# Projecting the queries' last 64 rows as row-tiled pairs, six tiles to a bank, in a recurrent-memory transformer kernel

## The chip, the cores and the metric

The kernel runs on one core of a Trainium2 chip. The metric is the device time of one execution in microseconds; the time before is the median of three runs. A profiled execution of the same program gives the trace.

## The reference

Two layers of a memory-augmented attention block and a gated feed-forward block, over 2048 tokens of 448 features. The attention block goes through 64 segments of 32 tokens one after another, because the first 8 output rows of a segment are the memory of the next:

```
for s in range(64):
    h = concat([mem, x[:, 32*s:32*s+32]])          # 40 rows of 448
    q, k, v = h @ Wq, h @ Wk, h @ Wv               # 16 heads of 256
    p = softmax(where(mask, q @ k.T / 16, -1e9))
    o = (p @ v) @ Wo
    mem, out_s = o[:, :8], o[:, 8:]
x = x + attention(layernorm(x)); x = x + (relu(g @ W_gate) * (g @ W_up)) @ W_down   # g = layernorm(x), twice
```

## The kernel before

The prologue multiplies the weights together per head: A = Wq Wk^T (448 x 448) and B = Wv Wo. So scores are (h A) h^T and the output is (p h) B, and k and v are never formed. A is kept in A_sb: the 448 input rows are four parts of 128 rows, the fourth having 64 rows and zeros. Heads come in two halves (hf 0 and 1) of eight. The 448 output rows of eight heads make 28 tiles of 128 (NT), numbered t; tiles 24 to 27 hold two heads' last 64 rows each.

Two chains run side by side, layer one at segment g and layer two at segment g - 4 (LAG). A step g handles both: 68 steps, of which g = 4 to 63 have both chains and 80 moving columns (two times 40), the others one chain and 40. After every second step a Feed (odd g) runs the feed-forward block of 64 tokens per layer.

TensorE's instructions are issued strictly in the order in which the program names them (`in_order`, line 73). The other engines' order is set by the scheduler when the program is built, and each engine then works through its own list in that order. PSUM has eight banks: seven in rotation (tag "ps") and one (tag "ox", bufs=1) that gathers the step's output.

One step on TensorE, in order: `project` of half 0 (h A, 28 tiles times four parts, evacuated to TQ and TZ by VectorE and ScalarE, groups of four tiles and 320 columns); `hk_make` (transposes h); `project` of half 1 with `scores_m(0)` (scores of the memory rows, tile Sm) between; `flipped` (transposes PM, the memory rows' probabilities, through PSUM tile pps into PT); `scores_x` (Sx: first a matmul that writes the mask, then 16 of 40 columns); `weigh_m` (ya, yb, from PT); the same for half 1; `project_out` (ox, 28 tiles times four); `weigh_x` (the other rows' y, from 40-row operands that sit on rows 0 to 39 and 64 to 103). At the end of a step `finish` reads ox: VectorE copies the new memory into the next h (`set_mem`, line 193), ScalarE copies the rest to OT (line 606).

`weights_of` (line 479) is the softmax: maximum (mx), subtraction (se), exponential on ScalarE, sum (ssum), reciprocal (rs), product.

The last part of h stands twice, on rows 0 to 63 and again on 64 to 127 (B_sb has 512 columns for that). `project_early` (line 434) uses it: eight of the 56 last-part matmuls of the next step, for tiles u = 6 and u = 0 of half 0, are issued as four pairs on upper and lower 64 rows, inside `weigh_x`, before the step's first full matmul. The other 48 are full-height matmuls over 64 rows of weights and 64 rows of zeros, in `project` (line 449).

Of the kernel before, what the change touches and what calls it, by code (L numbers as in the profile page):

```python
# [19 lines left out]
MEM = 8  # L20
# [13 lines left out]
W = 2 * L  # L34
XO = (0, 2 * L - SEG)
M0 = SEG
HX = (0, 64 + MEM)
HM = (SEG, 64)


EARLY = (6, 0)


def upper(hf, u):

    return hf == 0 and u == 0

# [6 lines left out]
def build_kernel(ctx, tc, A_x, A_mem0, A_Wq, A_Wk, A_Wv, A_Wo, B_W_gate, B_W_up, B_W_down, out,  # L54
# [79 lines left out]

    A_sb = glob.tile([P, 4, 2, NT, 128], BF, name="A_sb")
    B_sb = glob.tile([P, 2, NT, 512], BF, name="B_sb")
# [59 lines left out]
    with tc.tile_pool(name="pre", bufs=6) as pre:  # L196
# [4 lines left out]
        for i in range(6):  # L201
            t = pre.tile([P, 4, 512], BF, name=f"nat{i}", bufs=1)
            (nc.gpsimd if i % 2 else nc.vector).memset(t[64:128, 3, :], 0.0)
            nats.append(t)
        nc.gpsimd.memset(A_sb[64:128, 3, :, :, :], 0.0)
        nc.gpsimd.memset(A_sb[0:64, 3, 0, 0:4, :], 0.0)
        for t in TQ + TZ + PX + PM + YB:
# [60 lines left out]
        for p in range(NP):  # L268
# [4 lines left out]
            for kd in range(4):  # L273
                for eo in range(2):
                    aps = psum.tile([P, 3, 128], F32, tag="ps", name="aps")
                    for t in range(2):
                        e = 2 * eo + t
                        mm(aps[:, :, :], qT[:, e, kd * 128:(kd + 1) * 128],
                           kT[:, e, 0:384], start=(t == 0), stop=(t == 1))
                    for t in range(2):  # L280
                        e = 2 * eo + t
                        mm(mx_ps[:, kd, eo * 64:eo * 64 + 64], qT[:, e, kd * 128:(kd + 1) * 128],
                           kT[:, e, 384:448], start=(t == 0), stop=(t == 1))
                    t0 = eo * 4 + p4
                    if kd < 3:
                        share(A_sb[:, kd, hf, t0:t0 + 17:8, :], aps[:], 384, (1.28, 0.85))
                    elif upper(hf, eo):
                        share(A_sb[64:128, 3, hf, t0, :], aps[64:128, 0, :], 128, (1.28, 0.85))
                        share(A_sb[0:64, 3, hf, t0 + 8:t0 + 17:8, :], aps[0:64, 1:3, :], 256, (1.28, 0.85))
                    else:  # L290
                        share(A_sb[0:64, 3, hf, t0:t0 + 17:8, :], aps[0:64], 384, (1.28, 0.85))
                if todo:
                    todo.pop(0)()
            share(A_sb[:, 0:3, hf, 24 + p4, :], mx_ps[:, 0:3, :], 384, (1.28, 0.85))
            share(A_sb[0:64, 3, hf, 24 + p4, :], mx_ps[0:64, 3, :], 128, (1.28, 0.85))
            if p == 2:
# [55 lines left out]
    Wd_sb = main.tile([P, FT, DM], BF, name="Wd_sb")  # L352
    for dst, src in ((Wg_sb, B_W_gate), (Wu_sb, B_W_up)):
        nc.gpsimd.memset(dst[64:128, 3, :], 0.0)
        nc.sync.dma_start(dst[:, 0:3, :], src[0:384].rearrange("(k p) n -> p k n", p=P))
        nc.sync.dma_start(dst[0:64, 3, :], src[384:448])
    nc.sync.dma_start(Wd_sb[:], B_W_down.rearrange("(f p) d -> p f d", p=P))

# [74 lines left out]

    def project_early(chains, hb, j):

        n = L * len(chains)
        pre = {u: psum.tile([P, 512], F32, tag="ps", name="prj") for u in EARLY}
        low = [(u, p4) for u in EARLY for p4 in range(4) if not upper(0, u)]
        up = [(u, p4) for u in EARLY for p4 in range(4) if upper(0, u)]
        seen = set()  # L440
        for pair in zip(low, up):
            for u, p4 in pair:
                rows = slice(64, 128) if upper(0, u) else slice(0, 64)
                mm(pre[u][:, p4 * n:(p4 + 1) * n], A_sb[rows, 3, 0, 4 * u + p4, :],
                   moving(hb, j, 3, chains, rows), start=(u not in seen), stop=False, skip_group_check=True)
                seen.add(u)
        return pre

    def project(hf, chains, hb, j, us, pre={}):

        n = L * len(chains)
        for u in us:
            ps = pre[u] if u in pre else psum.tile([P, 512], F32, tag="ps", name="prj")
            for p4 in range(4):
                for kd in range(3 if u in pre else 4):
                    mm(ps[:, p4 * n:(p4 + 1) * n], A_sb[:, kd, hf, 4 * u + p4, :], moving(hb, j, kd, chains),
                       start=(kd == 0 and u not in pre), stop=(kd == (2 if u in pre else 3)),
                       skip_group_check=u in pre)
            if u < 6:
                parts = [(nc.scalar if u % 2 else nc.vector, slice(0, P), TQ[hf][:, :, u, :])]  # L460
            else:
                parts = [(nc.vector, slice(0, 64), TZ[hf][0:64, :, 0:64]),
                         (nc.scalar, slice(64, 128), TZ[hf][64:128, :, 64:128])]
            for eng, rows, T in parts:
                T = T.rearrange("p g (t q) -> p t g q", q=16)
                if len(chains) == 2:
                    evac(eng, T, ps[rows, 0:4 * n].rearrange("p (t g q) -> p t g q", t=4, q=16))
                    continue
                c = chains[0]
                src = ps[rows, 0:4 * n].rearrange("p (t w) -> p t w", t=4)  # L470
                x, m = (0, SEG) if c == 0 else (MEM, 0)
                evac(eng, T[:, :, 2, MEM * c:MEM * c + MEM], src[:, :, m:m + MEM])
                evac(eng, T[:, :, 3 * c:3 * c + 2, :],
                     src[:, :, x:x + SEG].rearrange("p t (g q) -> p t g q", q=16))

    def queries(hf, g, kd):
        return TQ[hf][:, g, 2 * kd:2 * kd + 2, :] if kd < 3 else TZ[hf][:, g, :]

    def weights_of(Sp, n, dst, keep, tag):

        mx = main.tile([P, n], F32, tag=f"mx{tag}", name="mx")
        nc.vector.tensor_reduce(mx[:], Sp[:], axis=AX.X, op=ALU.max)
        se = main.tile([P, n, L], F32, tag=f"se{tag}", name="se")
        nc.vector.tensor_tensor(se[:], Sp[:], mx[:].unsqueeze(2).to_broadcast([P, n, L]), op=ALU.subtract)  # L484
# [20 lines left out]
    def step(g, ff, pre):  # L505
# [6 lines left out]
        lo, hi = min(a for a, _ in cols), max(b for _, b in cols)  # L512
        ox = psum.tile([P, 4, W], F32, tag="ox", bufs=1, name="ox")

# [18 lines left out]
        def scores_x(hf):  # L533
            Sp = psum.tile([P, 4, L], F32, tag="ps", name="Sx")
            mm(Sp[:, :, :], ident[:], maskS[:], start=True, stop=False, skip_group_check=True)
            for half in range(2):
                for c in chains:
                    for kd in range(4):
                        mm(Sp[:, 2 * half + c, :], queries(hf, 3 * c + half, kd), moving(hb, j, kd, (c,)),
                           start=False, stop=(half == 1 and c == chains[-1] and kd == 3), skip_group_check=True)  # L540
            return Sp

        def probs_x(hf, Sp):
            weights_of(Sp, 4, PX[hf], None, f"x{hf}")

# [13 lines left out]
        def weigh_x(hf, hk, PT, then=None):  # L559

            def keep(eng, c, t0, src):
                n = src.shape[-1] // SEG
                dst = YB[hf][:, t0:t0 + n, XO[c]:XO[c] + SEG]
                k = max(1, n // 8)
# [26 lines left out]
        def project_out(hf, t0, t1):  # L591

            for t in range(t0, t1):
                for mc in range(4):
# [4 lines left out]
        def finish():  # L599
            if ms:  # L600
                src = ox[:, :, M0:M0 + 16].rearrange("p k (c m) -> p k c m", m=MEM)
                set_mem(g + 1, src[:, :, ms[0]:ms[-1] + 1, :], ms)
            o = (g - 1) % BLK * SEG
            for c in xs:
                o2 = o + (TB if c == 0 else 0)
# [12 lines left out]

        project(0, chains, hb, j, (6, 0, 1), pre)
        if ff is not None:  # L620
            ff.residual()
        project(0, chains, hb, j, (2, 3, 4, 5))
        hk = hk_make()
        if ff is not None:
            ff.norm()
        project(1, chains, hb, j, (6, 0, 1))
        scores_m(0)
        project(1, chains, hb, j, (2, 3))
        if ff is not None:
            ff.xposed()  # L630
        project(1, chains, hb, j, (4, 5))
        pm = flipped(PM[0], 1, "m0")
        Sx0 = scores_x(0)
# [4 lines left out]
        feed(0, 1, 2)  # L638
        project_out(0, 0, 18)
        probs_x(1, Sx1)  # L640
        pm = flipped(PM[1], 1, "m1")
        px0 = flipped(PX[0], 2, "x0")
        project_out(0, 18, 21)
        weigh_m(1, hk, pm)
        feed(3, 4)
        project_out(0, 21, NT)
        feed(5, 6)
        weigh_x(0, hk, px0)
        if ff is not None:
# [3 lines left out]
        if ff is not None:  # L653
            ff.norm2()
        project_out(1, 16, 25)
        if ff is not None:
            ff.feed_on()
        project_out(1, 25, NT)
        finish()
        nxt = active(g + 1)  # L660
        return weigh_x(1, hk, px1, (lambda: project_early(nxt, hTb[(g + 1) // BLK % 2], (g + 1) % BLK)) if nxt else None)


    nsteps = nseg + LAG

    pre = {}
    for g in range(nsteps + 1):
# [70 lines left out]
```

## Time and profile before

| what | us |
|---|---|
| median of three runs | 1717.07 (1716.97 to 1718.64) |
| profiled execution, its own time | 1716.17 |
| its span, first to last instruction | 1714.4 |
| TensorE busy | 1686.5 (98%) |
| VectorE busy | 1132.2 (66%) |
| ScalarE busy | 660.8 (39%) |
| first projection of step 0 starts at | 81.5 |

In the profile a row of a group has the line, engine and operation, what it writes and reads, the shape and the count, then busy us, mean ns of one, the engine's idle time before it and what ended that. Nearly all matmuls come from one helper (line 82), so they are told apart by their tiles: prj is the query projection, ox the output projection, Sm and Sx the scores, pps a transposition of probabilities, y, ya and yb the weighted rows, ups, gps and dps the feed-forward block. A timeline row has the start, the length, and the same names; rows that follow each other are merged.

### The profile page before, as it was taken

Reading aid. Unit: us, or ns where it says so; the run is one execution under the profiler, and the core shown is the slowest. Engines: PE = TensorE matmul, PEld = TensorE weight load, DVE = VectorE, ACT = ScalarE, POOL = GpSimd, SP = SyncE. Lnnn points to the kernel's source line nnn. Section 1 sums busy time; section 2 is a strip of 40 time slices with the busy share of each in tenths; the row PEclk is TensorE's granted clock in tenths of the full one; section 3 lists DMA queues with packets and bytes.
Section 4 is the critical chain, followed back from the end, with each engine's and each line's share of the span. In section 5 each row is a group of like instructions: output and inputs, shape, how many; then the busy total and the mean of one; then the engine's idle time right before and its main releaser. Section 6 shows DMA issues by size and latency. Waiting matters only on the chain.

```text
span 1714.4 us, 90663 instructions
## 1 busy us (share of the span) xinstructions
PE 1686.5 (98%) x41498; PEld 1589.5 (93%) x41498; DVE 1132.2 (66%) x3794; ACT 660.8 (39%) x1965; POOL 94.6 (6%) x202
## 2 busy tenths in 40 slices
PE   8989999999999999999999999999999999999998
PEld 6688999999999999999999999999999999999987
DVE  6656666676666666766666666766666667666664
ACT  5633333433333333343333334333333343433332
POOL 5300000000000000000000000000000000000000
PEclk9979999999999999999999999999999999999999
DMA  9520000000000000000000000000000000000000
GB/s 252 163 68 8 8 9 6 6 9 9 9 9 9 9 9 4 9 9 8 9 9 9 9 6 7 9 9 9 9 8 9 9 3 9 9 8 6 6 6 6
DMA packets 26623, 33.17 MB, mean 19 GB/s; under 512 B 3192, under 2 KB 24576, under 8 KB 26240
## 3 DMA queue, kind: packets, MB, share of 16 engines
q1 hardware_dynamic: 25152, 23.70, 5.0%
q8 instruction: 324, 5.31, 1.2%
q0 software_dynamic: 1088, 3.68, 0.7%
q14 instruction: 59, 0.48, 0.1%
HBM read 23.70 MB, written 1.84 MB: 15 GB/s over the span
## 4 chain that ended last, share of the span: by engine, by line
PE 96%; DVE 2%; issue 1%; ACT 1%; DMA 0%; POOL 0%; SPq 0%; POOLq 0%; DVEq 0%; ACTq 0%
PE ox L82 31%; PE prj L82 30%; PE ups L82 6%; PE gps L82 6%; PE dps L82 5%; PE y L82 4%; PE Sx L82 3%; PE pps L85 1%; PE bps L82 1%; PE tpw L85 1%; PE Sm L82 1%; PE aps L82 1%; PE ya L82 1%; PE tps L85 1%; PE yb L82 1%; PE kps L85 1%
## 5 line engine op out<-in xcount | busy, mean ns | idle before, releaser
L82 PE MATMUL ox<-Y,B_sb 128*128 128x80 bf16 (+4 forms) x15456 | 590.6, 199 | 1.5 <-issue 1.5
L82 PEld LDWEIGHTS <-B_sb 128*128 128x128 bf16 x15456 | 564.1, 99 | 10.2 <-issue 0.2
L82 PE MATMUL prj<-hT,A_sb 128*128 128x80 bf16 (+3 forms) x15232 | 569.5, 199 | 3.2 <-issue 3.2
L82 PEld LDWEIGHTS <-A_sb 128*128 128x128 bf16 (+1 forms) x15232 | 544.1, 99 | 7.8 <-issue 3.6
L89 ACT CAST TQ<-prj 128x320 bf16<-128x320 f32 (+1 forms) x456 | 169.9, 384 | 160.5 <-PE prj L82 128.5
L91 DVE CAST TQ<-prj 128x320 bf16<-128x320 f32 (+1 forms) x456 | 193.1, 431 | 44.9 <-PE prj L82 38.6
L91 DVE CAST Y<-y 128x128 bf16<-128x128 f32 (+2 forms) x384 | 162.2, 464 | 56.3 <-PE y L82 34.3
L89 ACT CAST Y<-y 128x512 bf16<-128x512 f32 (+2 forms) x384 | 144.2, 417 | 80.7 <-PE y L82 54.7
L396 DVE SCALAR_TENSOR_TENSOR hh<-gps,ut 128x256 bf16<-128x256 f32 (+1 forms) x238 | 95.6, 402 | 100.3 <-PE gps L82 93.6
L499 DVE COPY PT<-pps 128x128 bf16<-128x128 bf16 (+1 forms) x272 | 63.8, 255 | 120.2 <-PE pps L85 114.0
L82 PE MATMUL ups<-xT,Wu_sb 128*128 128x128 bf16 (+1 forms) x1904 | 140.0, 217 | 0.5 <-DVE xT L382 0.5
L82 PE MATMUL gps<-xT,Wg_sb 128*128 128x128 bf16 (+1 forms) x1904 | 140.0, 217 | 0.0
L395 ACT CAST ut<-ups 128x256 bf16<-128x256 f32 (+1 forms) x238 | 84.3, 355 | 105.5 <-PE ups L82 100.2
L557 ACT CAST Y<-yb 128x192 bf16<-128x192 f32 x134 | 42.6, 318 | 189.6 <-PE yb L82 189.0
L82 PEld LDWEIGHTS <-hk 40*128 40x128 bf16 (+1 forms) x1950 | 96.4, 95 | 16.9 <-issue 1.3
L82 PEld LDWEIGHTS <-Wg_sb 128*128 128x128 bf16 x1904 | 111.8, 98 | 0.0
L82 PEld LDWEIGHTS <-Wu_sb 128*128 128x128 bf16 x1904 | 109.5, 98 | 0.6 <-issue 0.6
L485 ACT ACTIVATE se<-se 128x80 f32<-128x80 f32 (+1 forms) x270 | 74.5, 299 | 90.0 <-DVE se L484 87.6
L160 POOL TENSOR_SCALAR rstd<-mv 128x1 f32<-128x1 f32 x67 | 14.8, 221 | 1554.1 <-DVE mv L158 1504.2
L82 PE MATMUL dps<-Wd_sb,hh 128*128 128x448 bf16 x476 | 95.9, 353 | 0.0
L82 PEld LDWEIGHTS <-TQ 128*128 128x128 bf16 x1938 | 86.8, 97 | 0.2 <-ACT TQ L89 0.2
L89 ACT CAST TZ<-prj 64x320 bf16<-64x320 f32 (+2 forms) x152 | 56.0, 378 | 74.2 <-DVE TZ L91 72.9
(112 smaller groups left out, 1801.1 us busy)
## 6 DMA issues: line engine op xcount, KB each, us to landing
wo<-in_A_Wo_dram POOLq DMA_DIRECT2D x8, 448.0 KB, 5.3
nat<-in_A_Wq_dram SPq DMA_DIRECT2D x8, 384.0 KB, 5.5
nat<-in_A_Wk_dram SPq DMA_DIRECT2D x8, 384.0 KB, 5.9
nat<-in_A_Wv_dram SPq DMA_DIRECT2D x8, 384.0 KB, 5.4
xa<-in_A_x_dram SPq DMA_DIRECT2D x32, 56.0 KB, 2.2
xa<-xp SPq DMA_DIRECT2D x32, 56.0 KB, 1.9
out_dram<-xa SPq DMA_DIRECT2D x32, 56.0 KB, 2.0
xp<-in_A_x_dram SPq DMA_DIRECT2D x30, 56.0 KB, 2.1
```

The lines of the kernel that those rows point to most:

```text
L82: in_order(nc.tensor.matmul(*a, **k))
L85: in_order(nc.tensor.transpose(*a))
L89: nc.scalar.copy(dst, src)
L91: eng.tensor_copy(dst, src)
L160: nc.gpsimd.tensor_scalar(out=rstd[:], in0=mv[:, 1:2], scalar1=EPS, scalar2=None, op0=ALU.add)
L395: nc.scalar.copy(ut[:, :, n], ups[:, :, n])
L396: nc.vector.scalar_tensor_tensor(out=hh[:, 2 * u:2 * u + 2, n], in0=gps[:, :, n], scalar=0.0, in1=ut[:, :, n], op0=ALU.max, op1=ALU.mult)
L485: nc.scalar.activation(se[:], se[:], AF.Exp, scale=SCALE)
L499: nc.vector.tensor_copy(PT[:], pps[:].rearrange("p b q -> p (b q)"))
L557: nc.scalar.copy(YB[hf][:, 16:28, M0:M0 + 16], yb[:].rearrange("p (t q) -> p t q", q=16))
```

## The change

- All 56 last-part matmuls of a step become 28 pairs (upper and lower 64 rows). Their weights move to a tensor of their own, A_tl, with half the tiles on each half of the rows; A_sb shrinks to three parts and its zeroing goes.
- Tiles are regrouped: bank b of a half holds tiles b, 4+b, ..., 20+b (six tiles, 480 columns); b = 4 holds tiles 24 to 27. So a half has five groups where it had seven, and evacuations are 480 columns wide.
- The pairs are issued in two groups: NEXT (12 pairs, banks 0 to 3 of half 0) where `project_early` was, with (0,3) in the ox bank; REST (16 pairs) after the full matmuls of half 0's banks 0 to 3.
- In half 1 the order is bank 4, bank 0, `scores_m(0)`, banks 1 and 2, Feed's transposes, bank 3.
- Where both chains run, the mask is added by VectorE to se before the maximum, and no longer by a matmul.
- `project_out` of half 0 is cut at 21 and 24 instead of 18 and 21. Step 67 leaves its output projection to step 68, which does both in one, 64 columns wide.
- In the prologue the transposition work of the next heads is issued after positions 0, 2, 4 and 5 of eight instead of after each second one. The feed-forward weights are loaded in fifteen pieces, each released by a matmul of steps 0 to 2, instead of five loads at once.

```
-EARLY = (6, 0)
+NEXT = (((0, 0), (0, 1)), ((0, 2), (0, 3)))
+REST = (((1, 4), (0, 4)), ((1, 0), (1, 1)), ((1, 2), (1, 3)))
+def bank(b):
+    return [24 + k for k in range(4)] if b == 4 else [4 * u + b for u in range(6)]
+def tail(hf, b):
+    up = hf == 1 if b == 4 else b % 2 == 0
+    return slice(64, 128) if up else slice(0, 64), 24 if b == 4 else 12 * hf + 6 * (b // 2)
...
-                if todo:
-                    todo.pop(0)()
+                    if todo and 2 * kd + eo in (0, 2, 4, 5):
+                        todo.pop(0)()
...
+    def project_tails(g, pairs):
+        chains = active(g)
+        hb, j, n = hTb[g // BLK % 2], g % BLK, L * len(chains)
+        part = {}
+        for pair in pairs:
+            for key in pair:
+                own = {"tag": "ox", "bufs": 1} if key == (0, 3) else {"tag": "ps"}
+                part[key] = psum.tile([P, 512], F32, name="prj", **own)
+            for k in range(len(bank(pair[0][1]))):
+                for key in pair:
+                    rows, i0 = tail(*key)
+                    mm(part[key][:, k * n:(k + 1) * n], A_tl[rows, i0 + k, :], moving(hb, j, 3, chains, rows),
+                       start=(k == 0), stop=False, skip_group_check=True)
+        return part
...
+        if mask is not None:
+            nc.vector.tensor_tensor(se[:], Sp[:], mask, op=ALU.add)
+            Sp = se
         nc.vector.tensor_reduce(mx[:], Sp[:], axis=AX.X, op=ALU.max)
...
-        project(0, chains, hb, j, (6, 0, 1), pre)
+        for b in (0, 1):
+            project(0, chains, hb, j, pre, b)
         if ff is not None:
             ff.residual()
-        project(0, chains, hb, j, (2, 3, 4, 5))
+        next_piece()
+        for b in (2, 3):
+            project(0, chains, hb, j, pre, b)
+        pre = project_tails(g, REST)
+        project(0, chains, hb, j, pre, 4)
         hk = hk_make()
         if ff is not None:
             ff.norm()
-        project(1, chains, hb, j, (6, 0, 1))
+        project(1, chains, hb, j, pre, 4)
+        project(1, chains, hb, j, pre, 0)
+        next_piece()
         scores_m(0)
-        project(1, chains, hb, j, (2, 3))
+        for b in (1, 2):
+            project(1, chains, hb, j, pre, b)
         if ff is not None:
             ff.xposed()
-        project(1, chains, hb, j, (4, 5))
-        pm = flipped(PM[0], 1, "m0")
+        project(1, chains, hb, j, pre, 3)
+        pm = flipped(PM[0], 1, "m0") if ms else None
         Sx0 = scores_x(0)
         weigh_m(0, hk, pm)
...
-        project_out(0, 0, 18)
+        next_piece()
+        project_out(0, 0, 21)
...
-        return weigh_x(1, hk, px1, (lambda: project_early(nxt, ...)) if nxt else None)
+        return weigh_x(1, hk, px1, (lambda: project_tails(g + 1, NEXT)) if active(g + 1) else None)
```

## The prediction

> **What bounds the kernel now.** I read the page first, then the groups with shapes kept apart, then the waits, then the timeline of one steady step. The page gives the span and the chain that ended last:
>
> ```profile
> span 1714.4 us, 90663 instructions
> PE 96%; DVE 2%; issue 1%; ACT 1%; DMA 0%; POOL 0%; SPq 0%; POOLq 0%; DVEq 0%; ACTq 0%
> ```
>
> TensorE is the bound almost everywhere, so a saved matmul shows in full unless PE then waits. The groups give the prices used below (busy us and mean ns after the bar):
>
> ```profile
> L91 DVE CAST TQ<-prj 128x320 bf16<-128x320 f32 x360 | 174.3, 484 | 38.0 <-PE prj L82 31.9
> L89 ACT CAST TQ<-prj 128x320 bf16<-128x320 f32 x360 | 153.0, 425 | 146.3 <-PE prj L82 115.4 <-PE pps L85 28.1 <-PE tps L85 0.6
> L91 DVE CAST Y<-y 128x512 bf16<-128x512 f32 x128 | 88.2, 689 | 42.4 <-PE y L82 34.3
> L89 ACT CAST Y<-y 128x512 bf16<-128x512 f32 x128 | 76.1, 595 | 54.7 <-PE y L82 54.7
> ```
>
> The timeline (PE, then DVE, of one step without Feed) shows what covers the first softmax:
>
> ```profile
> 696.39 0.27 PE L82 MATMUL Sm<-hT,TQ 128*128 128x80 bf16 x3
> ...
> 696.54 2.46 PE L82 MATMUL prj<-hT,A_sb 128*128 128x80 bf16 x64
> 698.83 0.22 PE L85 MATMUL pps<-ident,PM 128*128 128x128 bf16 x1
> ```
> ```profile
> 696.74 0.24 DVE L482 TENSOR_REDUCE mx<-Sm 128x2 f32<-128x80 f32 x1 [0.23 <-PE Sm L82]
> 697.01 0.24 DVE L484 TENSOR_TENSOR se<-Sm,mx 128x80 f32<-128x80 f32 x1
> 697.31 0.49 DVE L91 CAST TQ<-prj 128x320 bf16<-128x320 f32 x1
> 697.72 0.23 DVE L487 TENSOR_REDUCE ssum<-se 128x2 f32<-128x80 f32 x1
> 697.98 0.17 DVE L489 RECIPROCAL rs<-ssum 128x2 f32<-128x2 f32 x1
> 698.18 0.16 DVE L491 TENSOR_TENSOR rs<-rs,blk 128x2 f32<-128x2 f32 x1
> 698.38 0.24 DVE L492 TENSOR_TENSOR PM<-se,rs 128x80 bf16<-128x80 f32 x1
> ```
>
> Two things are to be seen. 64 full matmuls of 80 columns start in 698.83 - 696.54 = 2.29 us, 35.8 ns apiece. And PM is ready at 698.62, about 0.05 us more reaches PE (PT's copy ends at 699.31, ya starts at 699.37), and the transpose that reads it starts at 698.83: only 0.16 us of cover is left over. A record on DVE overlaps the next by 0.08 us (the cast at 697.31 lasts 0.49, the next starts 0.41 later).
>
> The step's seam:
>
> ```profile
> 709.16 0.45 PE L82 MATMUL ox<-Y,B_sb 128*128 128x80 bf16 x8
> 709.54 0.61 PE L82 MATMUL y<-PT,hk 40*128 40x256 bf16 x10
> 709.99 0.31 PE L82 MATMUL prj<-hT,A_sb 64*128 64x80 bf16 x8
> ```
> ```profile
> 709.90 0.43 ACT L606 CAST OT<-ox 128x128 bf16<-128x128 f32 x2 [3.31 <-DVE hT L193]
> 710.22 0.60 ACT L89 CAST Y<-y 128x512 bf16<-128x512 f32 x1
> ```
>
> Eight half-height matmuls end 0.31 us after they start; with 0.195 for the last, their starts span 0.115 us: four pairs, 35 to 40 ns a pair, so a pair costs what one full matmul does. The last full ox starts at 709.16 + 0.45 - 0.20 = 709.41, y at 709.54: 0.13 instead of 0.036, so entering half-height mode costs 0.10. The next full weight load is at 710.23, 0.126 after the last pair: leaving costs 0.09. y and the early tails share one such visit.
>
> A steady step with both chains lasts 19.52 us without Feed and 29.07 with (set_mem's rows at 661.06, 690.13, 709.65). There are 60, half of each kind.
>
> **The change, part by part, per steady step.**
>
> *Tails.* 48 full-height tail matmuls go: 48 x 35.8 = 1.72 us. Eight more pairs join the seam's visit: 0.28. Sixteen pairs come in a second visit: 0.56 + 0.10 + 0.09 = 0.75. Net -0.69. The trace has only four pairs in a row. Bounds for a long row: 35 ns, or 50 if every half-height matmul needs the 25 ns at which the smallest full ones start (four of Sx, 40 columns, in 698.96 to 699.06). I take 35, the row of the thing itself.
>
> At this place a rule can be weighed. The Trainium skill, "TensorE: Matmul & The Clock Gate", section "Wait — 56ns, not 53.3ns?", says that starts never come closer than about 25 ns however few the columns. By it a pair costs 50 ns, 24 more pairs cost 0.36 us more, and this term is -0.33. This case's trace disagrees for pairs: eight starts in 0.115 us.
>
> *Mask.* Two mask matmuls go; each holds PE 0.07 (698.89 to the next Sx at 698.96). In the second Sx that is gained. In the first it comes back: from pps (698.83) over PT's copy to ya (699.37) takes 0.54 on DVE, and PE's work between falls to 0.06 + 16 x 0.025 = 0.46. Net -0.07. DVE gets two adds of 0.31 (as the subtraction over Sx), holding it 0.23 each, both ahead of the second half's PM. That PM has 0.13 of cover to spare today (PX and PM done at 702.6 to 702.7, pps at 702.84), and gets 0.43 more, since 84 matmuls of project_out run ahead of its transpose instead of 72: 0 taken, bounds 0 and +0.2.
>
> *The ox bank.* Tile (0,3) of the first group takes ox's only buffer, so its first tail waits for both OT copies; all of PE's queue stands behind it. They end at 709.90 + 0.43 = 710.33; with 0.05 to 0.08 to reach PE that is 710.40. PE gets there after six pairs and one, 709.99 + 0.21 = 710.20. Cost +0.20. The six banks of the second group are free in time: the last evacuation that they need ends some 1 us before.
>
> *The first softmax, the term that decides.* Evacuations become 480 columns wide. By the 320 and 512 rows: DVE 484 + 160 x 205/192 = 655 ns, holding DVE 0.57; ACT 425 + 160 x 170/192 = 567 ns, holding ACT 0.45 (records there overlap by 0.11). PE's cover between Sm and pps shrinks from 64 to 54 projection matmuls. In the built program DVE's order is: cast of (1,0), mx, se, ssum, cast of (1,2), reciprocal, rs, PM; ACT's: cast of (1,1), then exp. From Sm's first start = 0, without Feed:
> - (1,0) ends on PE and its cast starts at 0.20; mx 0.77; se 1.04 to 1.28.
> - (1,1)'s last matmul starts at 0.75, its cast at 0.99; exp 1.44 to 1.70.
> - ssum 1.73; the cast of (1,2) 1.88; reciprocal 2.45; rs 2.65; PM 2.84 to 3.08; PE can start 3.13.
> - PE arrives at 4 x 0.036 + 54 x 0.0358 = 2.07. It waits 1.05.
>
> With Feed, DVE also has, ahead of the cast of (1,0), TZ of (0,4) from -1.09, the hk copy, two xn and TZ of (1,4) (holding 0.39, 0.31, 0.31, 0.21, 0.39), so that cast starts at 0.52 and mx at 1.09; exp 1.63, ssum 1.93, cast 2.07, reciprocal 2.64, then xT's copy (0.33), rs 3.05, PM 3.25 to 3.48, PE 3.53. PE arrives at 2.07 + 0.225 (tps) = 2.30. It waits 1.23.
>
> Behind pps stand Sx, ya, yb, the second Sm: everything. Bounds: 0.8 (casts no longer than 320's) to 1.4.
>
> Sum without Feed: -0.69 - 0.07 + 0.20 + 1.05 + 0.02 (ya of the second half, 0.02 late behind PT) = +0.51. With Feed: -0.69 - 0.07 + 0.21 + 1.23 = +0.68. Thirty of each: +35.7 us.
>
> **Edges, once per run.**
> - Single-chain steps (0 to 3, 64 to 66): 40-column matmuls cost 25 ns, so less is saved (about 0.3) and PM is late likewise, but PE already waited there. -0.3 to +0.7 each; +0.4 taken: +3.
> - Step 67's projection goes: 224 matmuls in 5.6 us (1692.85). Step 68's widen from 32 to 64 columns, 25 to 29 ns: +0.8. The transposes of PX lose that cover; up to 0.7 and 0.9 come back: -3.4 (-4.9 to -1.9).
> - Prologue: kT's late copy stalls PE at each of eight heads' pairs (48.64: aps starts 0.6 after the matmul before it), 4.2 us in all. The last transposition now has two positions more to hide in. The load of a later Wq lands only just ahead: -3 (0 to -4.2). Zeroing A_sb on POOL goes; the wo loads behind it start earlier; nothing waits for them.
> - Weights: five loads become fifteen on SP, five a step, each released by PE. Behind them stand x loads and stores not due before step 3; first use is in step 3 too. PE stood, with nothing that the profile shows to wait for, during the old burst (waits; then a window with span, busy times, clock, DMA share, GB/s):
>
> ```profile
> PE prj L82 <- issue: 3.2, 1, 3.2
> PE ox L82 <- issue: 1.5, 1, 1.5
> ```
> ```profile
> 84.00:92.00 8.00, 4.81 (x151) 4.63 (x147) 3.73 (x19) 2.24 (x13) 5.99 (x5) 0.78 1.05 308
> ```
>
> The next window, 92 to 100, has the clock at 0.50. These stops took 4.7 us; the half clock some 3 (step 1 lasts 17.8 us, step 2 only 15.9, and part of step 0). With the burst spread out I take -5 (0 to -8).
>
> Edges -8.4. Total +27.3: span 1741.7, the profiled execution 1716.17 becomes 1743.5, and the median, 0.9 above it, 1744.
>
> **Rivals.**
> 1. *The casts and the softmax overlap better and PM is in time* (faster). Per step -0.69 - 0.07 + 0.20 = -0.56, sixty times -34, edges -8: 1675. It decides where the wait at pps falls under about 0.7 us (0.56 and an eighth of a us of edges). For it: today's chain fits with 0.16 spare. Against: two 0.57 casts and one of 0.45 stand in the chain by the order, and the cover shrinks 0.36. Chance 0.07.
> 2. *A long row of pairs is held to 25 ns a start*, as the Sx matmuls are: 24 x 15 ns = +0.36 a step, +22, 1766. For it: four pairs could have had their weights in advance. Against: their spacing is level from the second on. Chance 0.04. The rule of the Trainium skill named above would give just this.
> 3. *The second softmax is late too*, because both mask adds stand in front of it: 0.2 a step, +12, 1756. Its spare is 0.13 today, its cover grows 0.43. Chance 0.05.
>
> **How the numbers follow.** The forecast has 0.82; no change (within 0.2%, about what can be told from no change here) 0.02. The terms' bounds are +-0.2 a step (12 us) and +-5 at the edges: 1728 to 1762, which leaves out rival 1, most of 2 and no change. Slower 0.91, faster 0.07.
>
> **What would show it.** A wait of PE at pps for DVE's PM, 60 times at 1.0 to 1.2 us; PE at prj for ACT's OT, 0.2; ya for PT, 0.08. Pairs at 35 ns in rows of 24 and 32. Steps of about 20.0 and 29.75 us. PE idle without a releaser gone from 86 to 96 us. I am wrong if pps starts straight after (1,3), or if pairs spread to 50 ns.

## The result and the profile after

The changed kernel takes 1745.95 us in the median of four runs (1744.33 to 1746.95), the kernel before 1717.02 (1716.60 to 1718.64) beside it: 1.0166 times as long, with an interval of 1.0148 to 1.0183. The profiled execution has a span of 1742.2 us against 1714.4: 27.8 us more.

The span, and the chain that ended last:

```profile
span 1742.2 us, 89627 instructions
PE 84%; DVE 10%; ACT 4%; issue 1%; DMA 1%; SPq 0%; POOL 0%; POOLq 0%; ACTq 0%; DVEq 0%
```

Before, 96% of that chain ran over TensorE. Now 14% of it lies on VectorE and ScalarE, and TensorE is busy for 1655.2 us, 31 less than before: the work was saved, and more than that was lost in waiting. The waits (us in total, times, the longest):

```profile
PE pps L93 <- DVE PM L514: 68.1, 70, 1.2
...
PE prj L90 <- ACT OT L640: 1.1, 2, 0.5
```

One wait carries nearly all of it. The view counts it from the end of the matmul before, which lies 0.2 us after that matmul's start. From start to start, less the usual 0.036, it is 1.07 us in a step without Feed and 1.27 with. The waits for OT and PT in steady steps are shorter than those 0.2 us and so hardly show in this view; they are read from starts, below.

The evacuations of six tiles, in the groups with shapes kept apart (busy us, mean ns of one, idle before):

```profile
L99 DVE CAST TQ<-prj 128x480 bf16<-128x480 f32 x240 | 156.2, 651 | 29.9 <-PE prj L90 19.2
L97 ACT CAST TQ<-prj 128x480 bf16<-128x480 f32 x240 | 133.9, 558 | 153.0 <-PE prj L90 151.1 <-PE otp L93 1.1
```

The whole first softmax of one step without Feed, in the timeline of VectorE, then ScalarE, then TensorE (start, length; the casts on VectorE are those of (1,0) and (1,2), the one on ScalarE is that of (1,1)):

```profile
1001.37 0.66 DVE L99 CAST TQ<-prj 128x480 bf16<-128x480 f32 x1
1001.95 0.23 DVE L505 TENSOR_REDUCE mx<-Sm 128x2 f32<-128x80 f32 x1
1002.21 0.24 DVE L506 TENSOR_TENSOR se<-Sm,mx 128x80 f32<-128x80 f32 x1
1002.92 0.24 DVE L509 TENSOR_REDUCE ssum<-se 128x2 f32<-128x80 f32 x1 [0.47 <-ACT se L507]
1003.08 0.65 DVE L99 CAST TQ<-prj 128x480 bf16<-128x480 f32 x1
1003.64 0.15 DVE L511 RECIPROCAL rs<-ssum 128x2 f32<-128x2 f32 x1
1003.83 0.16 DVE L513 TENSOR_TENSOR rs<-rs,blk 128x2 f32<-128x2 f32 x1
1004.02 0.24 DVE L514 TENSOR_TENSOR PM<-se,rs 128x80 bf16<-128x80 f32 x1
1004.59 0.23 DVE L521 COPY PT<-pps 128x128 bf16<-128x128 bf16 x1 [0.33 <-PE pps L93]
```
```profile
1002.16 0.56 ACT L97 CAST TQ<-prj 128x480 bf16<-128x480 f32 x1 [0.46 <-PE prj L90]
1002.62 0.27 ACT L507 ACTIVATE se<-se 128x80 f32<-128x80 f32 x1
```
```profile
1001.31 2.10 PE L90 MATMUL prj<-hT,A_sb 128*128 128x80 bf16 x54
1004.32 0.23 PE L93 MATMUL pps<-ident,PM 128*128 128x128 bf16 x1 [0.91 <-DVE PM L514]
```

Three casts stand in this chain. mx starts, without idling before it, when the cast of (1,0) lets go (1001.95); exp only when the cast of (1,1) on ScalarE does (1002.62, se having ended at 1002.45); the reciprocal only when the cast of (1,2) does (1003.64, ssum having ended at 1003.16). TensorE's 54 matmuls started before 1003.25; pps starts at 1004.32.

The seam and the second visit to half-height mode, in TensorE's timeline, and OT in ScalarE's:

```profile
994.92 0.61 PE L90 MATMUL y<-PT,hk 40*128 40x256 bf16 x10
995.37 0.77 PE L90 MATMUL prj<-hT,A_tl 64*128 64x80 bf16 x24
996.07 2.75 PE L90 MATMUL prj<-hT,A_sb 128*128 128x80 bf16 x72
998.75 0.75 PE L90 MATMUL prj<-hT,A_tl 64*128 64x80 bf16 x32
999.43 0.60 PE L90 MATMUL prj<-hT,A_sb 128*128 128x80 bf16 x12
```
```profile
995.28 0.43 ACT L640 CAST OT<-ox 128x128 bf16<-128x128 f32 x2
```

The 16 pairs take 999.43 - 998.75 = 0.68 us with 0.13 for leaving, so 0.55 over 15 distances: 36 ns a pair. The 12 pairs take 0.70; at 36 ns they would take 0.53. The other 0.17 to 0.18 is one distance, from the first matmul of the second pair of tiles to its partner in tile (0,3): it waits for OT, which ends at 995.71.

Steady steps went from 19.52 and 29.07 us to 20.06 and 29.80 (starts of set_mem). The sixty of them together, from the set_mem that ends step 3 to the one that ends step 63, went from 1452.8 to 1490.5: +37.7 us. The edges give 9.9 back.

### The profile page after: what moved, and what is told of

Read it like the earlier page. It is cut to its first block, busy times and chain, and to the rows that moved or that the text cites. A ratio compares the mean times of both kernels' runs of the same rounds, so it can differ in the third digit from the quotient of the medians.

```text
span 1742.2 us, 89627 instructions
## 1 busy us (share of the span) xinstructions
PE 1655.2 (95%) x41152; PEld 1534.2 (88%) x41152; DVE 1143.5 (66%) x3766; ACT 643.0 (37%) x1803; POOL 88.3 (5%) x200
## 4 chain that ended last, share of the span: by engine, by line
PE 84%; DVE 10%; ACT 4%; issue 1%; DMA 1%; SPq 0%; POOL 0%; POOLq 0%; ACTq 0%; DVEq 0%
PE ox L90 30%; PE prj L90 21%; PE ups L90 6%; PE gps L90 6%; PE dps L90 5%; PE y L90 4%; PE Sx L90 3%; DVE TQ L99 2%; PE pps L93 2%; ACT TQ L97 2%; PE bps L90 1%; PE ya L90 1%; DVE ssum L509 1%; DVE TZ L99 1%; PE tpw L93 1%
## 5 line engine op out<-in xcount | busy, mean ns | idle before, releaser
L90 PE MATMUL prj<-hT,A_sb 128*128 128x80 bf16 (+1 forms) x11424 | 450.6, 200 | 0.0
L90 PEld LDWEIGHTS <-A_sb 128*128 128x128 bf16 x11424 | 417.2, 100 | 8.3
L97 ACT CAST TQ<-prj 128x480 bf16<-128x480 f32 (+2 forms) x304 | 147.5, 496 | 167.7 <-PE prj L90 165.6
L99 DVE CAST TQ<-prj 128x480 bf16<-128x480 f32 (+2 forms) x304 | 171.6, 572 | 35.6 <-PE prj L90 24.5
L507 ACT ACTIVATE se<-se 128x80 f32<-128x80 f32 (+1 forms) x270 | 80.2, 304 | 87.9 <-DVE se L506 86.0
L99 DVE CAST TZ<-prj 64x320 bf16<-64x320 f32 (+2 forms) x152 | 63.3, 424 | 65.8 <-PE prj L90 65.8
L90 PE MATMUL prj<-hT,A_tl 64*128 64x80 bf16 (+1 forms) x3808 | 101.0, 196 | 1.1 <-ACT OT L640 1.1
L93 PE MATMUL pps<-ident,PM 128*128 128x128 bf16 x134 | 30.4, 227 | 68.2 <-DVE PM L514 68.1
```

What stands on the lines that cost most here:

```text
L90: in_order(nc.tensor.matmul(*a, **k))
L93: in_order(nc.tensor.transpose(*a))
L97: nc.scalar.copy(dst, src)
L99: eng.tensor_copy(dst, src)
L507: nc.scalar.activation(se[:], se[:], AF.Exp, scale=SCALE)
```

## The experiments

All start from the changed kernel unless said otherwise; the step times are starts of set_mem to starts of set_mem.

**1. The wait taken away by other data.**

```
-        pm = flipped(PM[0], 1, "m0") if ms else None
+        pm = flipped(PM[1], 1, "m0") if ms else None
```

> The changed kernel, but the first transposition of memory probabilities reads PM[1], left by the step before, in place of PM[0]: it no longer has anything to wait for (the values are wrong, the work is the same). Theory (the casts of 480 columns stand in VectorE's list between Sm and PM): the waits at pps of 1.07 and 1.27 us go, but PT's copy still stands in the same list behind the cast of (1,2), the reciprocal and rs. Without Feed rs starts at 1003.83, so PT would run from 1003.91 to 1004.13 and PE have it at 1004.18, where PE without the wait is at ya at 1003.72: 0.46 of waiting at ya instead of 0.075. With Feed the same sum gives 0.68. Gain 0.69 and 0.66 a step, 40 us: 1706 (1698 to 1714), with the waits at ya for PT at 0.45 and 0.65. Rival (the wait is the softmax's own chain of dependent results, whatever stands between): with the data there at once nothing is left to wait for, 70 us less: 1676. Rival (the loss sits in the pairs or the cover, not in this wait): stays above 1735.

Measured: 1695.7 us, 0.9879 of the kernel before (0.9864 to 0.9893), steps 19.33 and 29.11, so 0.73 and 0.69 less. In a step without Feed:

```profile
878.41 0.22 PE L93 MATMUL pps<-ident,PM 128*128 128x128 bf16 x1
...
879.34 0.27 PE L90 MATMUL ya<-PT,hk 128*128 128x128 bf16 x2 [0.31 <-DVE PT L521]
```
```profile
878.24 0.65 DVE L99 CAST TQ<-prj 128x480 bf16<-128x480 f32 x1
...
878.99 0.16 DVE L513 TENSOR_TENSOR rs<-rs,blk 128x2 f32<-128x2 f32 x1
879.07 0.22 DVE L521 COPY PT<-pps 128x128 bf16<-128x128 bf16 x1
```

pps starts straight after the projection, it is done at 878.63, and the copy starts at 879.07: that stands behind the cast of (1,2) in VectorE's list. ya starts 0.49 after the matmul before it, where 0.10 was seen in the changed kernel (0.69 with Feed). So a queue and not only a chain of results is behind the wait, as the first theory had it to 0.04 us a step. The total of 1695.7 lies below the expected range of 1698 to 1714. The sixty steady steps gave 42.5 us, where 40 were expected. The sum had left out the single-chain steps, which wait in the same way: steps 1 to 3 and 64 to 66 became 5.8 us shorter, and step 0 1.3.

**2. Full-height tails, all else as changed.**

```
-    A_sb = glob.tile([P, 3, 2, NT, 128], BF, name="A_sb")
-    A_tl = glob.tile([P, NT, 128], BF, name="A_tl")
+    A_sb = glob.tile([P, 4, 2, NT, 128], BF, name="A_sb")
...
-            for k in range(len(bank(pair[0][1]))):
-                for key in pair:
-                    rows, i0 = tail(*key)
-                    mm(part[key][:, k * n:(k + 1) * n], A_tl[rows, i0 + k, :], moving(hb, j, 3, chains, rows),
-                       start=(k == 0), stop=False, skip_group_check=True)
...
-            for kd in range(3):
+            for kd in range(4):
...
```

> The changed kernel with the pairs alone undone: A_sb has its fourth part of 64 rows and zeros again, project runs four full-height matmuls a tile, no tail is issued ahead; banks of six tiles, casts of 480 columns, the order, mask, prologue and weights stay as changed. Per step PE gains 28 x 35 ns = 0.98 of pairs, 0.19 of the second visit's switching and the 0.145 of waiting for OT, and pays 56 x 35.8 ns = 2.00: +0.69. Theory (pps waits because PE comes to it too early): 18 of the 56 stand between Sm and pps, and with PE slower ScalarE's list has exp before the cast of (1,1) and VectorE's has PM before the cast of (1,2). From Sm = 0: cast of (1,0) 0.20, mx 0.77, se 1.04, exp 1.31, ssum 1.60, reciprocal 1.86, rs 2.06, PM 2.25 to 2.48, PE could start at 2.53; it arrives at 0.144 + 72 x 0.0358 = 2.72 (2.94 with Feed). No wait at pps, about 0.08 to 0.18 more at ya: -1.07 + 0.69 + 0.05 and -1.27 + 0.69 + 0.1, so 0.33 and 0.48 a step less, 24 us: 1722 (1712 to 1730). Rival (the wider casts alone make the wait, whatever PE does): 0.64 more cover leaves 0.43 and 0.63 of waiting, so 0.05 a step more than the changed kernel: 1749.

Measured: 1715.25 us, 0.9993 (0.9984 to 1.0002), steps 19.60 and 29.32. The wait at pps is gone from steady steps, as this part of the waits shows (nine times in all, at the edges):

```profile
PE pps L93 <- DVE PM L507: 4.5, 9, 0.8
```
```profile
888.34 0.23 DVE L502 TENSOR_REDUCE ssum<-se 128x2 f32<-128x80 f32 x1 [0.34 <-ACT se L500]
...
889.00 0.24 DVE L507 TENSOR_TENSOR PM<-se,rs 128x80 bf16<-128x80 f32 x1
889.16 0.65 DVE L99 CAST TQ<-prj 128x480 bf16<-128x480 f32 x1
```

With a slower TensorE, the list that was written for VectorE has PM before the cast of (1,2). The casts are as wide as in the changed kernel, and pps no longer waits; what is left is ya waiting for PT, 0.09 us without Feed and 0.26 with. So the width alone does not make the loss. Doing *more* work on TensorE made a step 0.46 and 0.48 us shorter. This also shows that the order on the other engines is not a given when TensorE's work changes.

**3. The order alone.**

```
+                if hf == 1 and b in (1, 2):
+                    tc.add_manual_dep(r.ins, held[b],
+                                      mybir.DependencyInfo(mybir.DependencyClass.NoSync,
+                                                           mybir.DependencyReason.DATA),
+                                      reason="softmax first")
...
+        if tag == "m0":
+            held[1] = r.ins.name
...
+        if tag == "m0":
+            held[2] = r.ins.name
```

r is the cast, held[1] the first softmax's exp and held[2] its last product, PM.

> The changed kernel with the engines as they are and the order alone altered: ScalarE's cast of (1,1) is put behind exp and VectorE's cast of (1,2) behind PM. Only the cast of (1,0) stays in front. From Sm's start: that cast 0.20, mx 0.77, se 1.04, exp 1.31, ssum 1.60, reciprocal 1.86, rs 2.06, PM 2.25, PE 2.53; it arrives at 2.07: a wait of 0.46 instead of 1.07. With Feed the copy of xT (0.33) now comes in front of rs: about 3.1 against 2.30, 0.8 instead of 1.27. PT stands behind the cast of (1,2): ya waits 0.25 instead of 0.075. Gain 0.43 and 0.29 a step, 22 us: 1724 (1716 to 1733). Rival (order does not matter, only how much work VectorE has in this stage): no change, 1746.

Measured: 1723.99 us, 1.0042 (1.0028 to 1.0056), steps 19.60 and 29.51: 0.46 and 0.29 less than the changed kernel, 22 us in all, as worked out. VectorE's rows now run straight from ssum to PM:

```profile
892.69 0.23 DVE L516 TENSOR_REDUCE ssum<-se 128x2 f32<-128x80 f32 x1 [0.34 <-ACT se L512]
892.96 0.17 DVE L518 RECIPROCAL rs<-ssum 128x2 f32<-128x2 f32 x1
...
893.35 0.24 DVE L521 TENSOR_TENSOR PM<-se,rs 128x80 bf16<-128x80 f32 x1
893.51 0.65 DVE L99 CAST TQ<-prj 128x480 bf16<-128x480 f32 x1
894.08 0.22 DVE L530 COPY PT<-pps 128x128 bf16<-128x128 bf16 x1
```

From the start of bank (1,3)'s last matmul to that of pps it is now 0.54 us instead of 1.11; from the last Sx to ya 0.25 instead of 0.10, since PT stands behind the moved cast. The same work in another order recovers 22 of some 70 us; the cast of (1,0) and, with Feed, xT still stand in front. Two casts were moved at once, (1,1) on ScalarE and (1,2) on VectorE; no run tells their shares apart.

**4. Half 1's casts on ScalarE.**

```
-            parts = [(nc.scalar if b % 2 else nc.vector, slice(0, P), T)]
+            parts = [(nc.scalar if hf or b % 2 else nc.vector, slice(0, P), T)]
```

> The changed kernel with the casts of all four six-tile banks of half 1 on ScalarE (before: banks 0 and 2 on VectorE). Theory (the two casts of 480 columns in VectorE's list make PM late): from Sm's start mx 0.35, se 0.62, exp 0.89 (behind the cast of (1,0), 0.24 to 0.80), ssum 1.18, reciprocal 1.44, rs 1.63, PM 1.83 to 2.06, PE can start at 2.11; it arrives at 2.07. The wait at pps falls to 0.04 without Feed and to nothing with it. What comes next: the second Sm waits for ScalarE's cast of (1,3) by 0.05 to 0.1. Gain 1.0 and 1.2 a step, 65 us: 1681 (1672 to 1692), faster than before. Rival (the softmax's own steps are too long for 54 matmuls): the wait stays above 0.4: 1715 or more. Rival (ScalarE becomes late: its list is then four casts of 0.45 and exp): a wait of over 0.5 at the second Sm, 1705 or more.

Measured: 1689.36 us, 0.9840 (0.9825 to 0.9855), faster than the kernel before. Steps 19.19 and 28.80: 0.87 and 1.00 less, where 1.0 and 1.2 were expected. What was missed is on ScalarE:

```profile
873.90 0.42 ACT L97 CAST TZ<-prj 64x320 bf16<-64x320 f32 x1
874.35 0.56 ACT L97 CAST TQ<-prj 128x480 bf16<-128x480 f32 x1
874.80 0.27 ACT L507 ACTIVATE se<-se 128x80 f32<-128x80 f32 x1
```
```profile
874.41 0.24 DVE L506 TENSOR_TENSOR se<-Sm,mx 128x80 f32<-128x80 f32 x1
...
875.77 0.24 DVE L514 TENSOR_TENSOR PM<-se,rs 128x80 bf16<-128x80 f32 x1
```

se is done at 874.65, exp starts at 874.80. The cast of (1,0) before it had begun late, because TZ's cast kept ScalarE for 0.45 us: the next instruction started 0.02 after that cast's end, and not 0.10 before it, as exp did after the cast of (1,0) (874.35 + 0.56 to 874.80). The same 0.02 follows this cast of TZ in the kernel before and in the changed kernel. So pps still waits 0.21 and 0.25 us. The rival in which ScalarE becomes the bound did not come: the second Sm waits at most 0.13.

**5. OT from another source.**

```
-                nc.scalar.copy(OT[:, :, o2:o2 + SEG], ox[:, :, XO[c]:XO[c] + SEG])
+                nc.scalar.copy(OT[:, :, o2:o2 + SEG], YB[1][:, 0:4, XO[c]:XO[c] + SEG])
```

> The changed kernel, but the two copies to OT at a step's end read YB[1] (SBUF) and not ox; the outputs are wrong, the copies have the same shape. So tile (0,3) of the next step, which takes ox's bank, waits for set_mem alone, which ends long before. Theory (the thirteenth tail matmul waits for the OT copies, and everything on PE behind it): the distance there falls from 0.181 us to 0.035, 0.145 a step, sixty times 8.7: 1737 (1734 to 1741). By the prediction's 0.20 it would be 1734. Rival (the stop belongs to the pairs' second tile, or to another bank, and not to OT): the distance stays, 1746.

Measured: 1730.69 us, 1.0083 (1.0068 to 1.0099): 15.3 less than the changed kernel, where 8.7 were expected, and below the range of 1734 to 1741. The seam in TensorE's timeline:

```profile
887.37 0.61 PE L90 MATMUL y<-PT,hk 40*128 40x256 bf16 x10
887.82 0.59 PE L90 MATMUL prj<-hT,A_tl 64*128 64x80 bf16 x24
888.35 1.82 PE L90 MATMUL prj<-hT,A_sb 128*128 128x80 bf16 x46
```

The 12 pairs now take 0.53 instead of 0.70. My 0.145 had taken the usual distance inside a pair to be 35 ns; here two partners start 3 to 4 ns apart, so the whole 0.18 was waiting, and the prediction's 0.20 was nearer. With Feed the step became 0.23 shorter, as the wait at pps fell by another 0.06; the sixty steps gave 11.9 us. Steps 1 to 3 and 64 to 66, left out of my sum, gave 1.8. That is 13.7 of the 14.2 us between the two profiled executions; the rest is small and lies at the edges.

**6. The two edge parts on the kernel before.**

```
-                if todo:
-                    todo.pop(0)()
+                    if todo and 2 * kd + eo in (0, 2, 4, 5):
+                        todo.pop(0)()
...
+        next_piece()
```

next_piece, as in the change, stands at five places of a step, and the five loads at once are gone.

> The kernel before with two parts of the change alone: the transposition work of the prologue after positions 0, 2, 4 and 5, and the feed-forward weights in fifteen pieces released by matmuls of steps 0 to 2. Steps are otherwise those of before. Theory (the edges' gain is in the prologue and the weights): the end of step 0 comes 8 us earlier, as in the changed kernel (94.5 instead of 102.7), and stays so: 1708.5 (1706 to 1712). By the prediction's terms the prologue is 3 of this and the weights 5. Rival (the gain at the edges comes with the pairs in the single-chain steps): under 3 us, 1714 or more.

Measured: 1707.74 us, 0.9952 (0.9937 to 0.9967). The first projection starts at 78.93 instead of 81.46: 2.5 us from the prologue. Step 0 from there to its set_mem takes 94.77 - 78.93 = 15.84 instead of 102.67 - 81.46 = 21.21: 5.4 us, put down to the weights because that is where their loads ran. The split goes by place; no run has one of the two edits without the other. The windows from 84 us on (span, then busy times of PE, PEld, DVE, ACT and POOL, clock, DMA share, GB/s), with the two of the kernel before that follow the one shown in the prediction:

```profile
84.00:92.00 8.00, 7.14 (x219) 6.53 (x216) 5.88 (x31) 3.27 (x12) 3.55 (x3) 0.94 0.36 119
92.00:100.00 8.00, 8.00 (x228) 7.74 (x226) 2.55 (x13) 2.27 (x11) 0.00 (x0) 0.50 0.47 148
100.00:108.00 8.00, 7.07 (x228) 6.68 (x225) 6.82 (x35) 3.01 (x14) 0.00 (x0) 0.92 0.30 91
```

Before:

```profile
92.00:100.00 8.00, 6.49 (x170) 6.01 (x168) 4.57 (x22) 2.33 (x7) 0.00 (x0) 0.50 0.31 96
100.00:108.00 8.00, 8.00 (x227) 7.74 (x225) 2.49 (x13) 2.27 (x10) 0.00 (x0) 0.50 0.02 5
```

TensorE's stops are gone (7.14 of 8 us busy where it was 4.81, and 8.00 where it was 6.49). The half clock is not gone, but it is shorter. Taking the clock as either full or half, the mean of 0.78 from 84 to 92 puts its start at about 88.5 before, and 0.78 from 100 to 120 its end at about 108.8: some 20 us. In this run 0.94 and 0.92 put it from about 91.0 to 101.3: some 10 us. Nearly all of the difference lies in step 0, so how the 5.4 us divide between the stops and the clock stays open. Step 1 begins with some 6 us of half clock in both, and lasts 17.9 us here and 17.8 before.

**7. The mask by matmul.**

```
-            if not both:
+            if True:
                 mm(Sp[:, :, :], ident[:], maskS[:], start=True, stop=False, skip_group_check=True)
...
-            weights_of(Sp, 4, PX[hf], None, f"x{hf}", maskS[:] if len(chains) == 2 else None)
+            weights_of(Sp, 4, PX[hf], None, f"x{hf}", None)
```

> The changed kernel with the mask written by a matmul again in every step, and no add on VectorE. The second Sx is 0.07 longer, of which the wait of the second half's ya (0.02) gives back a little; the first Sx is 0.07 longer too, but ya's wait for PT (0.075) goes for it. So 0.05 a step more, 3 us: 1749 (1746 to 1752). Rival (the two adds of 0.23 on VectorE cost more than the matmuls saved, because a later softmax or cast waits behind them): faster than the changed kernel, 1741 or less.

Measured: 1749.09 us, steps 20.12 and 29.87, 0.06 and 0.07 more than the changed kernel. About 0.05 was expected. The first ya no longer waits for PT (0.031 us behind the last Sx instead of 0.10), and the second half's ya follows project_out as closely as in the changed kernel. The adds on VectorE cost nothing that shows.

**8. A mended version.** Experiment 4, and with it:

```
-        hk = hk_make()
...
+        got = []
+        project(1, chains, hb, j, pre, 1, lambda: got.append(hk_make()))
+        hk = got[0]
...
         Sx0 = scores_x(0)
+        feed(0)
         weigh_m(0, hk, pm)
...
-                nc.scalar.copy(OT[:, :, o2:o2 + SEG], ox[:, :, XO[c]:XO[c] + SEG])
+                r = nc.vector.tensor_copy(OT[:, :, o2:o2 + SEG], ox[:, :, XO[c]:XO[c] + SEG])
+                held["ot"] = r.ins.name
```

The function handed to project is called after three of the bank's six tiles; VectorE's casts of y in half 1 are put behind held["ot"].

> The changed kernel with the late PM mended from both sides, and three small waits with it. All casts of half 1's six-tile banks on ScalarE, as in the run before, where steps last 19.19 and 28.80 and pps still waits 0.21 and 0.25, because exp stands behind the cast of (1,0) on ScalarE. New: h's four transpositions (0.22 of PE) go from before the first Sm into the middle of bank (1,1), so Sm starts 0.22 earlier and the cover grows by as much: the wait at pps goes (Sm itself then waits some 0.03 for TZ). OT is copied by VectorE straight behind set_mem: the ox bank is free 0.08 earlier. feed(0) stands between the first Sx and ya, so with Feed ya (0.07) and the second Sm (0.125) wait no more; without Feed the second Sm waits 0.08 for the cast of (1,3). Without Feed 19.19 - 0.21 - 0.08 + 0.08 + 0.03 = 19.01; with Feed 28.80 - 0.25 - 0.08 - 0.19 + 0.03 = 28.31. Thirty of each: 20 us less than the run before, 1669 (1662 to 1678). Rival (ScalarE's list is the next bound): steps stay near 19.2 and 28.8, 1685 or more.

Measured: 1665.95 us (1665.16 to 1666.89), 0.9707 of the kernel before (0.9692 to 0.9721). Steps 18.95 and 28.47. Its span and chain, and VectorE in a step without Feed:

```profile
span 1663.6 us, 89640 instructions
PE 96%; DVE 2%; ACT 1%; issue 0%; DMA 0%; POOL 0%; SPq 0%; POOLq 0%; DVEq 0%; ACTq 0%
```
```profile
861.40 0.24 DVE L508 TENSOR_TENSOR se<-Sm,mx 128x80 f32<-128x80 f32 x1
861.68 0.39 DVE L547 COPY hk<-kps 128x448 bf16<-128x448 bf16 x1
862.05 0.23 DVE L511 TENSOR_REDUCE ssum<-se 128x2 f32<-128x80 f32 x1
...
862.71 0.24 DVE L516 TENSOR_TENSOR PM<-se,rs 128x80 bf16<-128x80 f32 x1
863.35 0.23 DVE L523 COPY PT<-pps 128x128 bf16<-128x128 bf16 x1 [0.39 <-PE pps L94]
```

The copy of hk fills the gap in which VectorE waits for exp, PM is ready at 862.95, and pps starts at 863.09 without a wait. The chain lies on TensorE again, with the share that it had before. At the seam the wait for OT is 0.11 instead of 0.18: 0.07 gained.

**9. The mended version with full-height tails.** The edit is that of experiment 2.

> The last mended kernel (1666 us, steps of 18.95 and 28.47) with the pairs undone: full-height tails over 64 rows of zeros, nothing else changed. What are the pairs worth where no softmax waits for them? Theory: their whole price in PE time. A step pays 56 x 35.8 ns = 2.00, and saves 28 pairs x 35 ns = 0.98, the second visit's switching 0.19 and the wait for OT 0.11: 0.72 more, 43 us in sixty steps, and some 0.3 in each of seven single-chain steps: 1711 (1705 to 1717). Steps of 19.67 and 29.19. Rival (in the mended kernel another engine is the bound, so the pairs' time is hidden): under 20 us more, 1686 or less. Rival (it is the mending that gains and the pairs are worth nothing): 1666.

Measured: 1702.94 us, 0.9913 (0.9896 to 0.9929), steps 19.60 and 29.06. The total lies just below the expected range of 1705 to 1717. The pairs are worth 0.65 and 0.59 us a step there, 37 us in all, where 0.72 a step and 43 in sixty were expected; nor did the single-chain steps become longer, as had been expected. Why the pairs saved a little less than their price stays open. Its steps are nearly those of the kernel before (19.52 and 29.07), so its 14 us of gain over that kernel lie at the edges. In the steady steps, then, nearly all that the change has to give is in the pairs, and the order and place of the casts decide whether it is seen.

## Why the prediction was right

- *The first softmax, +1.05 and +1.23.* Measured 1.07 and 1.27. With mx's start put at the predicted 0.77, the rows shown give exp 1.44, ssum 1.74, cast of (1,2) 1.90, reciprocal 2.46, PM 2.84 and pps 3.14, where 1.44, 1.73, 1.88, 2.45, 2.84 and 3.13 were predicted. The widths came out at 651 and 558 ns (655 and 567 were extrapolated). It was the built order of VectorE's and ScalarE's lists, and not the diff, that gave this: experiments 3 and 4 shorten the wait by moving casts, experiment 1 moves most of it to ya by taking PM out of it, and experiment 2 shows the same casts in another order without it.
- *Tails, -0.69, and mask, -0.07.* A step without Feed grew by 0.54; the new waits in it are 1.07 (pps), 0.18 (OT) and 0.07 (first ya), 1.32 in all, so TensorE's own time fell by 0.78 (0.79 with Feed). The prediction's two terms give 0.69 + 0.14, the mask's counted before ya's wait. Pairs cost 36 ns (35 taken). Experiment 7 has the mask at 0.06 to 0.07. The 0.02 put down for the second half's ya did not come: it starts 0.036 behind the matmul before it in both kernels.
- *The ox bank, +0.20.* 0.18 by starts, and by experiment 5.
- *Rival 1, PM in time:* it did not come in this kernel, but its sum was near what PM in time is worth: experiment 8, which brings that about and saves a few small waits besides, gains 35.0 us over the kernel before in the sixty steady steps, where the rival had 34. That it takes 1666 us and not the rival's 1675 comes from the edges. *Rival 2, 25 ns a start:* refuted by 36 ns a pair in rows of 12 and 16. The Trainium skill, "TensorE: Matmul & The Clock Gate", section "Wait — 56ns, not 53.3ns?", says that starts never come closer than about 25 ns, however few the columns. For such pairs that does not hold here: two matmuls on different halves of the rows start 3 to 4 ns apart. *Rival 3, second softmax late:* in the steady steps the second half's pps starts 0.036 us behind the last matmul of project_out, without a wait.
- *Edges, -8.4.* Measured -9.9. The first projection comes 3.5 earlier (3 predicted; 2.5 in experiment 6). The weights' term was right in size, 5.4 against 5. Its working was right only in part: the stops went, but of the half clock, part of the bound of 8, some 10 of 20 us stayed, as experiment 6 shows. Single-chain steps cost 2.5 by the set_mem rows and experiment 6 (3 predicted), the end saves 3.4 (42.1 to 38.7 us from the last set_mem, as predicted, though the terms listed there give 3.2 to 4.8, and the 1.9 at the end of that range is not worked out).
- The steady sum was 35.7 and is 37.7; the edges' error goes the other way. So 27.3 predicted against 27.8 is closer than its terms, and that last half microsecond is luck.

## What to carry to other kernels

When TensorE's work between a result and its use shrinks, list what the other engines do in that time, in the order in which their lists were built, and lay the new durations along it; a saving of 0.69 us became a loss because three casts stood in front of a softmax that had 0.16 us to spare. A saving that turns into a wait is not lost: look which instructions in front of the late one need not be there, move them to an engine that idles, or move work of TensorE's into the gap. Compare several orders, since a change on TensorE alone may also change the lists of the others.

## What the runs showed of the hardware

- Two half-height matmuls on the upper and the lower 64 rows start 3 to 4 ns apart, and a row of 16 such pairs of 80 columns keeps 36 ns a pair, with 0.10 us for entering the mode and 0.10 for leaving it. Behind the wait for OT the partners soon start 16 to 20 ns apart, and a pair still takes 36.
- In experiment 6, where the burst of weight loads (DMA share 1.05, 308 GB/s in one window) is spread out, TensorE's unexplained stops are gone, and the half clock that follows is shorter, some 10 us instead of 20 (10 to 14 in the changed kernel and its variants, which spread the loads too). It is not gone: the clock is 0.50 from 92 to 100 us also with a DMA share of 0.47. Why it falls there, and why for less long, is open; no run was made on it.
- ScalarE's next instruction starts 0.10 us before the end of a 480-column cast of 128 rows, but 0.02 after the end of a 320-column cast of 64 rows (experiment 4). What decides it was not tried.
